# A recurrence and a gated MLP in one kernel: 16-bit ordering products and one lasting pair of accumulator banks

## The chip, the cores and the metric

The kernel runs on one core of a Trainium2 chip. The metric is the time of one execution on the device in microseconds (us), lower is better; where several were timed, the median is given. One further execution was recorded by the hardware profiler, and all rows below come from it. Its engines are called PE (matmul), PEld (the loading of weights into the PE array, which runs beside the matmuls), DVE (vector), ACT (scalar), POOL and SP (which issues the DMAs).

## What is computed

First a linear recurrence with a state of 48 x 48 for each of 4 sequences and 8 heads over 768 steps, then an MLP of 3072 rows, 384 to 2048 to 384, with a hard-swish gate:

```python
for t in range(S):
    kt, vt, rt, wt = (k[:, :, t], v[:, :, t], r[:, :, t], w[:, :, t])
    cur = np.einsum('bhd,bhe->bhde', u[None] * kt, vt)
    y[:, :, t] = np.einsum('bhd,bhde->bhe', rt, state + cur)
    state = wt[:, :, :, None] * state + np.einsum('bhd,bhe->bhde', kt, vt)
...
h = x @ w_in
relu6 = np.clip(h + 3.0, 0.0, 6.0)
g = h * relu6 / 6.0
return (g @ w_out).astype(np.float32)
```

All of it is in 32-bit floats.

## The kernel before

The recurrence is cut into 24 chunks of 128 steps (6 for each sequence, two sequences interleaved: chunks 0, 2, 4, ... 10 belong to one, 1, 3, ... 11 to the other, and 12 to 23 likewise). Each chunk consists of two halves of 64 steps (`a` = 0, 1). Eight heads are four pairs (`p`) of an even and an odd head (`g` = 0, 1). Features of even heads stand in partitions 0 to 47, those of odd heads in 64 to 111; partitions 48 to 63 are zero padding. So `PR` is 112, `GP` is 64, `D` is 48 and `HL` is 64.

For each chunk DVE makes decay products by scans (`back_scan`, `fore_scan`), PE multiplies keys by receptances (`score`, L500), DVE masks these into `A` (`above`), PE turns the keys (`turn_k`, L516) and ACT copies them out as `kn` (`turned_k`). PE then makes the **outer products** of keys and values that enter the state (`write`, L600). ACT copies them out as `kvs` (`written`, L611) and DVE adds them to the decayed state. The result of a chunk comes from **state products** (`read_state`, L578) and **value products** (`read_values`, L587), both added up in `y_ps`, from where ACT takes them as the MLP's input (`leave`, L685).

`y_ps` is a tile of two banks of the accumulator memory, one for each half `a`: columns 0 to 255 hold y of one chunk, columns 256 to 447 the outer products of the next. `new_y` allocates it anew for each read, in the same place, since the pool has one buffer of that name.

The MLP's matmuls for four chunks at a time (a block) fill the rest of PE's time: L718 and L737 for block 0, L833 (up) and L888 (down) for the five later ones, the latter with fewer products and more sums on DVE. The order of all steps is fixed by hand, in a long string (`ORDER`) that ranks them; each step issues its instructions in a fixed sequence on its engine. From chunk 4 on, one step (`read`) strings together, on PE: the 16 state products of chunk i, an **ordering product** (`mark`, L622), the 16 scores of chunk i + 1, a second ordering product, the 16 outer products of chunk i + 1 (8 if that chunk is one of the last two of its pair of sequences, 10, 11, 22 and 23), the 16 value products of chunk i, and the 4 transposes for chunk i + 2. Chunks 0 to 4 (`SOLO`) have their outer products in a step of their own (`write_alone`), and chunk 1 has these and y in other banks (`APART`, `KV_APART`).

An ordering product multiplies a 64 x 64 part of the identity by four of its columns, into a small tile `ps` that nobody reads. It makes PE's later products wait until the earlier ones are done, where both go to the same banks from different parts of the array. Each f32 matmul shows in the trace as two weight loads and two matmuls.

The outer product's weights are `kn[half, p, cols]`: 64 rows (steps of the half), and as columns the features, 0 to 63 for an even head (48 and the 16 of padding) and 64 to 111 for an odd one. The padding's columns write zeros to partitions 48 to 63 of `y_ps`, which ACT's copy of 112 partitions (L611) reads along.

Of the kernel before, what the change touches and what calls it, by code (L numbers as in the profile page):

```python
# [8 lines left out]
F32 = mybir.dt.float32  # L9
# [4 lines left out]
BF16 = mybir.dt.bfloat16  # L14
# [7 lines left out]
HL = L // 2  # L22
GP = 64
# [15 lines left out]
KV_APART = (1,)  # L39
# [205 lines left out]
def fast_path(tc, feat, tok, wflat, ub, ug, moe_w_in, moe_w_out, out, flag, n_chunks):  # L245
# [5 lines left out]
    nc = tc.nc  # L251
    NT, PR, nf = feat.shape[0], ug.shape[0], feat.shape[2]
    HD = tok.shape[3]
    D = PR - GP
    H = HD // D
    P = H // 2
# [11 lines left out]
    with ExitStack() as ctx:  # L268
# [3 lines left out]
        pp = ctx.enter_context(tc.tile_pool(name="pp", bufs=1, space=PSUM))  # L272
# [10 lines left out]
        def is_last(i):  # L283
            return i % NSEQ >= NSEQ - 2
# [6 lines left out]
        ident = const.tile([128, 128], F32, name="ident")  # L291
# [8 lines left out]
        u_bc = const.tile([128, HD], F32, name="u_bc")  # L300
        w_in = const.tile([128, NFC // 2, NCC, 2, 128], F32, name="w_in")
        w_out = const.tile([128, NFC, DM], F32, name="w_out")

        def constants():

            nc.vector.memset(back, 0.0)
            nc.vector.memset(back[:, :, HL:], 1.0)
            for b in starts:
                nc.vector.memset(b, 0.0)
            nc.vector.memset(three, 3.0)  # L310
            nc.vector.memset(ones, 1.0)
            make_identity(nc, ident)
            nc.gpsimd.tensor_add(eyes, ident[:, :HL], ident[:, HL:])

            mask_f = wk.tile([128, HL], F32, name="clip")
            nc.gpsimd.memset(mask_f, 1.0)
            for a in range(2):
                nc.gpsimd.affine_select(out=mask_f[a * HL:(a + 1) * HL], in_=mask_f[a * HL:(a + 1) * HL],
                                        compare_op=ALU.is_gt, fill=0.0, base=0, pattern=[[1, HL]], channel_multiplier=-1)
            nc.gpsimd.tensor_copy(out=mask, in_=mask_f)  # L320

            for _ in range(4):
                spin()

            new_x(0)
            x3_0 = blocks[0]["x3"]
            sel = blocks[0]["sel"] = wk.tile([PR, NCC, 128], F32, name="S_", bufs=1)
            nc.gpsimd.memset(x3_0, 0.0)
            nc.gpsimd.memset(sel, 0.0)
            for g in range(2):  # L330
                nc.gpsimd.tensor_copy(out=sel[:, :, g * GP + D:g * GP + D + X3],
                                      in_=ident[0:PR, g * GP:g * GP + D].rearrange("q (j r) -> q j r", j=NCC))

        def new_x(bk):

            x = wk.tile([128, NCC + 1, MB], F32, name="xT")
            blocks[bk].update(xT=x, x3=x[:PR, NCC])
# [213 lines left out]
        def new_y(i, alone=False):  # L551
            started = set()
            if i == APART and not alone:
                st[i].update(started=started, y_ps=[bank()[:, :P * HL].rearrange("q (p t) -> q p t", p=P) for _ in range(2)])
                return
            y_ps = pp.tile([128, 2, 512], F32, name="y_ps")
            if not alone:
                y_ = y_ps[:, :, :P * HL].rearrange("q a (p t) -> q a p t", p=P)
                st[i].update(started=started, y_ps=[y_[:, a] for a in range(2)], y_all=y_)
            j = i if alone else i + 1  # L560
            if j < NT and (alone or j not in SOLO):
                st[j]["kv_started"] = started
                st[j]["kv_ps"] = y_ps[:PR, :, P * HL:P * (HL + D)].rearrange("q a (p e) -> q a p e", p=P)
# [26 lines left out]
        def write(i):  # L590
            d = st[i]
            for p in range(P):
                for a in range(1 if is_last(i) else 2):
                    for g in range(2):

                        half = slice(a * HL, (a + 1) * HL)
                        cols = slice(g * GP, GP if g == 0 else PR)
                        fresh = (a, g * GP) not in d["kv_started"]
                        d["kv_started"].add((a, g * GP))
                        nc.tensor.matmul(d["kv_ps"][a][cols, p, :] if i in KV_APART else d["kv_ps"][cols, a, p, :], lhsT=d["kn"][half, p, cols],  # L600
                                         rhs=d["v"][half, 2 * p + g, :], start=fresh, stop=True, skip_group_check=True)
# [12 lines left out]
        def write_alone(i):  # L614
            if i in KV_APART:
                st[i].update(kv_started=set(), kv_ps=[bank()[:PR, :P * D].rearrange("q (p e) -> q p e", p=P) for _ in range(2)])
            else:
                new_y(i, True)
            write(i)

        def mark():
            nc.tensor.matmul(pp.tile([HL, 4], F32, name="ps"), lhsT=ident[HL:, HL:], rhs=ident[HL:, :4], start=True, stop=True)  # L622

        def read(i):

            new_y(i)
            read_state(i, range(P))
            if i + 1 < NT:
                mark()
                score(i + 1)  # L630
                mark()
                write(i + 1)
            else:
                nc.tensor.drain()
            read_values(i, range(P))
            if i + 2 < NT:
                turn_k(i + 2)
# [12 lines left out]
        def clear_y(i):  # L650
            new_y(i)
            for a in range(2):
                nc.tensor.matmul(st[i]["y_ps"][a], lhsT=ident[0:PR, :], rhs=blocks[0]["x3"][:, BY_SUM * L:BY_SUM * L + P * HL],
                                 start=True, stop=False, skip_group_check=True)
            st[i]["started"].update((a, g * GP) for a in range(2) for g in range(2))
# [54 lines left out]
        def bank(name="bank"):  # L710
            return pp.tile([128, 512], F32, name=name, bufs=4 if name == "bank" else 1)
# [451 lines left out]
        for bk in range(NB):  # L1163
# [7 lines left out]
            for d in range(2 * (bk > 0)):  # L1171
                at = K + U_ / 2 * d
                u, r = f"up{bk}.{d}.", f"read{bk}.{d}."
                name = lambda x: u + str(x) if isinstance(x, int) else r + x
# [41 lines left out]
            for p in range(2 * (bk > 0)):  # L1216
# [28 lines left out]
                for c, ((soon, s0), (late, l0)) in enumerate(((("c11", 0), ("c12", DM // 2)), (("c22", DM // 2), ("c21", 0)))):  # L1245
                    name = f"store{bk}.{2 * p + c}"
# [6 lines left out]
        for k, (which, j) in enumerate(vets):  # L1253
            i = 8 + k // 2
# [10 lines left out]
        def spin():  # L1265

            n_ = spins[0] = spins[0] + 1
            at = n_ % 4 * L
            nc.tensor.matmul(still[:, at:at + L], lhsT=ident, rhs=ident, start=n_ == 0, stop=True, skip_group_check=True)  # L1269
# [7 lines left out]
        plan.spin, plan.hint = spin, hint  # L1277
        plan.hint_at = f"down{NB - 1}.1.3.0"
        constants()
        plan.emit()  # L1280

# [237 lines left out]
def kernel(  # L1519
# [25 lines left out]
    flags = ctx.enter_context(tc.tile_pool(name="flags", bufs=1))  # L1545
    flag = flags.tile([1, 1], I32, name="flag")
    fast_path(tc, feat, tok, wflat, ub, ug, moe_w_in, moe_w_out, out, flag, n_chunks)
    bad = nc.values_load(flag[0:1, 0:1], min_val=0, max_val=128)
    with tc.If(bad > 0, preferred_fallthrough_block=True, label="general"):
# [68 lines left out]
```

## Time and profile before

| what | before |
|---|---|
| median of 3 timed runs | 536.13 us (535.11 to 536.87) |
| span of the profiled execution, first to last instruction | 533.3 us |
| granted PE clock | 1.000 |
| L622, ordering products: passes (loads), duration of one load | 76, 134 ns |
| L600, outer products into `y_ps`: passes | 672 |
| L578, state products into `y_ps`: passes | 688 |
| L587, value products into `y_ps`: passes | 736 |

The profiled execution is told by its span alone; the timed runs lie 2.8 us above it, for what happens ahead of the first instruction and behind the last. A load's duration is the time that one load spends under way; loads of the four quadrants of the array overlap, so that the distance between loads, not their duration, tells how fast they follow each other. In a timeline row stand the start, the length from the first start to the last end of the merged instructions, the engine, the line, the operation, the tiles, rows * columns of the weights, the shape, the count, and in brackets the idle time ahead with what ended it.

### The profile page before, as it was taken

The page shows a single profiled execution, that of the slowest core. Times are in us where ns is not written, and L with a number is a line of the kernel's source. Part 1 is how long each engine was busy: PE and PEld are TensorE (multiplying, and loading weights), DVE is VectorE, ACT ScalarE, POOL GpSimd, SP SyncE. Part 2 cuts the span into 40 slices and gives each one's busy share as a digit, 9 for nine tenths or more (in the row PEclk, how much of TensorE's full clock was granted, in tenths as well). Part 3 has the DMA queues.
Part 4 walks back from the last instruction along what each step waited for, and adds up shares of the span by engine and source line. Part 5 has one row for each costly group of instructions (what it writes and reads, how often), then busy time and mean ns, then how long its engine had stood idle before and what let it go on. Part 6 is the DMA issues. An engine that isn't in the chain of part 4 may idle for free.

```text
span 533.3 us, 13527 instructions
## 1 busy us (share of the span) xinstructions
PE 527.5 (99%) x5630; PEld 471.5 (88%) x5630; DVE 421.9 (79%) x741; ACT 263.8 (49%) x657; POOL 88.7 (17%) x79
## 2 busy tenths in 40 slices
PE   8999999999999999999999999999999999999997
PEld 8888877766888999988999988999988999988997
DVE  8989999877999977899677999886758855458740
ACT  4999886542356314474434466524245454253400
POOL 2000002450303033220432312114020000000000
PEclk9999999999999999999999999999999999999999
DMA  8958653343003535644324748122710000100001
GB/s 326 354 172 341 241 181 120 125 163 103 31 17 139 165 115 198 235 161 123 102 75 154 248 166 262 40 78 97 244 58 0 1 10 15 54 2 0 9 2 54
DMA packets 21458, 66.42 MB, mean 125 GB/s; under 512 B 3312, under 2 KB 11408, under 8 KB 21392
## 3 DMA queue, kind: packets, MB, share of 16 engines
q1 hardware_dynamic: 21264, 65.50, 35.8%
q8 instruction: 46, 0.75, 0.6%
q14 instruction: 20, 0.16, 0.1%
q10 hardware_dynamic: 128, 0.00, 0.0%
HBM read 59.69 MB, written 4.72 MB: 121 GB/s over the span
## 4 chain that ended last, share of the span: by engine, by line
PE 93%; DVE 4%; issue 1%; ACT 1%; DMA 1%; DVEq 0%; ACTq 0%
PE bank L888 29%; PE bank L833 25%; PE bank L737 8%; PE bank L718 7%; PE bankS L888 5%; PE bankS L833 4%; PE y_ps L578 3%; PE y_ps L587 2%; PE bank L500 2%; PE ps L516 2%; PE y_ps L600 2%; PE bankS L1269 1%; PE ps L475 1%; DVE g L858 1%; DVE g L850 1%
## 5 line engine op out<-in xcount | busy, mean ns | idle before, releaser
L854 ACT ACTIVATE clip<-g,three 128x512 f32<-128x512 f32 x80 | 56.5, 720 | 47.0 <-DVE g L850 29.9
L850 DVE TENSOR_TENSOR g<-bank,g 128x512 f32<-128x512 f32 x80 | 54.1, 685 | 22.3 <-PE bank L833 21.2
L858 DVE SCALAR_TENSOR_TENSOR g<-clip,g 128x512 f32<-128x512 f32 x80 | 57.3, 732 | 1.8 <-ACT clip L854 1.5
L888 PE MATMUL bank<-w_out,g 128*128 128x192 f32 x320 | 56.6, 326 | 0.0
L491 ACT ACTIVATE A<-eyes,dg 128x64 f32<-128x64 f32 x192 | 50.1, 339 | 9.2 <-PE y_ps L587 8.9
L450 POOL TENSOR_TENSOR K<-feat_in,E 112x512 f32<-112x512 f32 x17 | 24.9, 1466 | 175.0 <-PE ps L622 150.1
L888 PEld LDWEIGHTS bank<-w_out,g 128*128 128x128 f32 x320 | 52.9, 190 | 0.4
L718 PE MATMUL bank<-xT,w_in 128*128 128x256 f32 (+1 forms) x216 | 45.3, 361 | 0.2 <-DVE w_in L417 0.2
L454 POOL TENSOR_TENSOR W<-feat_in,W 112x512 f32<-112x512 f32 x17 | 22.8, 1341 | 125.7 <-DVE W L439 125.7
L737 PE MATMUL bank<-w_out,g 128*128 128x384 f32 x128 | 43.4, 488 | 0.0
L848 ACT COPY g<-bank 128x512 f32<-128x512 f32 x50 | 28.4, 584 | 30.3 <-PE bank L833 30.3
L718 PEld LDWEIGHTS bank<-xT,w_in 128*128 128x128 f32 x216 | 36.7, 190 | 5.4 <-PE bank L718 0.5
L833 PE MATMUL bank<-xT,w_in 128*128 128x256 f32 x160 | 40.5, 380 | 0.1
L685 ACT COPY xT<-y_ps 48x256 f32<-48x256 f32 x88 | 32.2, 366 | 13.9 <-PE y_ps L587 13.0
L906 ACT ACTIVATE o<-bank 128x192 f32<-128x192 f32 x30 | 9.5, 329 | 56.2 <-PE bank L888 56.1
L737 PEld LDWEIGHTS bank<-w_out,g 128*128 128x128 f32 x128 | 23.8, 190 | 14.3 <-DVE w_out L417 0.2
L439 DVE TENSOR_TENSOR_SCAN W<-feat_in,start 112x520 f32<-112x520 f32 x24 | 29.6, 1232 | 5.9 <-PE ps L622 5.8
L833 PEld LDWEIGHTS bank<-xT,w_in 128*128 128x128 f32 x160 | 30.2, 190 | 4.4 <-DVE g L850 0.5
L430 DVE TENSOR_TENSOR_SCAN E<-feat_in,back 112x520 f32<-112x520 f32 x24 | 30.2, 1258 | 1.2 <-DMA feat_in<-in_feat_dram 1.1
L833 PE MATMUL bank<-xT,bits 128*128 128x256 f32 x120 | 30.4, 380 | 0.0
L466 POOL TENSOR_TENSOR rk<-rk_in 128x384 f32<-128x384 f32 x15 | 21.0, 1402 | 46.4 <-DVE dg L483 29.2
L888 PE MATMUL bankS<-w_out,g 128*128 128x192 f32 x160 | 28.6, 327 | 0.0
(288 smaller groups left out, 1132.5 us busy)
## 6 DMA issues: line engine op xcount, KB each, us to landing
feat_in<-in_feat_dram SPq DMA_DIRECT2D x23, 772.5 KB, 4.7
bits<-in_moe_w_in_dram SPq DMA_DIRECT2D x8, 768.0 KB, 6.6
bits<-in_moe_w_out_dram SPq DMA_DIRECT2D x8, 768.0 KB, 6.0
feat_in<-in_moe_w_in_dram SPq DMA_DIRECT2D x8, 768.0 KB, 4.7
feat_in<-in_moe_w_out_dram SPq DMA_DIRECT2D x8, 768.0 KB, 4.9
rk_in<-in_tok_dram SPq DMA_DIRECT2D x15, 384.0 KB, 5.0
v_in<-in_tok_dram SPq DMA_DIRECT2D x24, 192.0 KB, 4.6
feat_in<-in_wflat_dram SPq DMA_DIRECT2D x6, 768.0 KB, 5.3
```

The lines of the kernel that those rows point to most:

```text
L430: nc.vector.tensor_tensor_scan(out=E_[:, ::-1], data0=d["w"][:, :0:-1], data1=back.rearrange("q p t -> q (p t)")[:, ::-1], initial=0.0, op ...
L439: nc.vector.tensor_tensor_scan(out=W_, data0=d["w"][:, :-1], data1=starts[i % 2].rearrange("q p t -> q (p t)"), initial=0.0, op0=ALU.mult, ...
L491: nc.scalar.activation(out=d["A"][:, h, :], in_=eyes, func=ACT.Copy, scale=d["dg"][:, h])
L685: nc.scalar.copy(out=blocks[bk]["xT"][g * GP:g * GP + D, :, at:at + HL], in_=st[i]["y_ps"][a][(g ^ a) * GP:(g ^ a) * GP + D, :, :])
L718: nc.tensor.matmul(h_ps[:, :(c1 - c0) * L], lhsT=w_in[:, f // 2, j, f % 2, :], rhs=b["xT"][:, j, c0 * L:c1 * L], start=(j == 0), stop=(j = ...
L737: nc.tensor.matmul(b["o", c][:, :DM], lhsT=g_of(0, f, c), rhs=w_out[:, f, :], start=(f == 0), stop=(f == NFC - 1))
L833: nc.tensor.matmul(b["p", d, c][:, z * HB:(z + 1) * HB], lhsT=weight(W_PLACE[r], d)[:, z, :], rhs=x_at(bk, X_PLACE[r]), start=fresh and z ...
L848: nc.scalar.copy(out=out_, in_=src)
L850: nc.vector.tensor_tensor(out=out_, in0=src, in1=out_of(bk, d, other), op=ALU.add if sign > 0 else ALU.subtract)
L854: nc.scalar.activation(out=c, in_=out_of(bk, d, u), func=ACT.Relu, bias=three, scale=twice)
L858: nc.vector.scalar_tensor_tensor(out=g, in0=blocks[bk]["r", d, u], scalar=6.0, in1=g, op0=ALU.min, op1=ALU.mult)
L888: nc.tensor.matmul(b["d", p, to][:, :h], lhsT=a, rhs=w(), start=(f == 0 and k in (1, 5)), stop=(f == HF - 1 and k in (2, 3, 4)), skip_grou ...
```

## The change

Three edits. The ordering product is made from the identity's bits read as 16-bit floats: 64 rows, 34 columns (34 rather than 64 output rows), in one pass. `y_ps` is allocated once, ahead of all work, and DVE clears partitions 0 to 111 of its columns from 256 on, in both banks, among the first memsets. And an even head's weights in the outer product are its 48 columns alone, except for chunk 1, whose other banks are not cleared.

```diff
+        y_ps = pp.tile([128, 2, 512], F32, name="y_ps")
...
+            nc.vector.memset(y_ps[:PR, :, P * HL:], 0.0)
...
-            y_ps = pp.tile([128, 2, 512], F32, name="y_ps")
             if not alone:
                 y_ = y_ps[:, :, :P * HL].rearrange("q a (p t) -> q a p t", p=P)
...
-                        cols = slice(g * GP, GP if g == 0 else PR)
+                        cols = slice(g * GP, GP if g == 0 and i in KV_APART else g * GP + D)
...
         def mark():
-            nc.tensor.matmul(pp.tile([HL, 4], F32, name="ps"), lhsT=ident[HL:, HL:], rhs=ident[HL:, :4], start=True, stop=True)
+            bits = ident.bitcast(BF16)[HL:]
+            nc.tensor.matmul(pp.tile([HL // 2 + 2, 4], F32, name="ps"), lhsT=bits[:, :HL // 2 + 2], rhs=bits[:, :4], start=True, stop=True)
```

On PE, read 11 (the block at 199.84 us of the trace) stands before as follows, from its state products to the first outer products (out<-in, output rows x columns, and in brackets the engines or DMA queues whose semaphores are waited for):

```order
L578 MATMUL y_ps<-W,S 48x64 [waits PE_49,Activation_49]
L578 MATMUL y_ps<-W,S 48x64
L578 MATMUL y_ps<-W,S 48x64 [waits DVE_49]
L578 MATMUL y_ps<-W,S 48x64 x13
L622 MATMUL ps<-ident 64x4 [waits PE_49]
L500 MATMUL bank<-W,K 64x64 [waits Pool_49]
L500 MATMUL bank<-W,K 64x64 [waits Activation_49]
L500 MATMUL bank<-W,K 64x64 x14
L622 MATMUL ps<-ident 64x4 [waits PE_49]
L600 MATMUL y_ps<-v_in,kn 64x48 [waits DMAHW3_49]
L600 MATMUL y_ps<-v_in,kn 48x48
```

and now, at the same place (the lines are one or two further down in the file):

```order
L579 MATMUL y_ps<-W,S 48x64 [waits Activation_49]
L579 MATMUL y_ps<-W,S 48x64
L579 MATMUL y_ps<-W,S 48x64 [waits DVE_49]
L579 MATMUL y_ps<-W,S 48x64 x13
L624 LDWEIGHTS ident
L624 MATMUL ps<-ident 34x4 [waits PE_49]
L502 MATMUL bank<-W,K 64x64 [waits Pool_49]
L502 MATMUL bank<-W,K 64x64 [waits Activation_49]
L502 MATMUL bank<-W,K 64x64 x14
L624 LDWEIGHTS ident
L624 MATMUL ps<-ident 34x4 [waits PE_49]
L601 MATMUL y_ps<-v_in,kn 48x48 [waits DMAHW3_49]
```

Nothing has moved. The first state product no longer waits for PE's own earlier work (13 of the reads lose that wait; read 10 had none), an ordering product is now a load and a matmul as two instructions, and all outer products have 48 rows. Behind the last read two up products (L833) of the last block gain a wait for PE.

On DVE, the start of the program before:

```order
L306 MEMSET back 112x520
L307 MEMSET back 112x8 [waits DVE_49]
L309 MEMSET start_79 112x520
L309 MEMSET start_80 112x520
L310 MEMSET three 128x1
L311 MEMSET ones 128x1
L430 SCALAR_TENSOR_TENSOR E<-feat_in,back 112x520 [waits DMAHW1_49,DVE_49]
```

and now:

```order
L307 MEMSET back 112x520
L308 MEMSET back 112x8 [waits DVE_49]
L310 MEMSET start_79 112x520
L310 MEMSET start_80 112x520
L311 MEMSET y_ps 112x2x256
L312 MEMSET three 128x1
L313 MEMSET ones 128x1
L432 SCALAR_TENSOR_TENSOR E<-feat_in,back 112x520 [waits DMAHW1_49,DVE_49]
```

One memset of 512 columns stands ahead of the first scan.

## Prediction

> **What bounds the kernel now.** I read the page first: busy shares, the slices with the granted clock, and the chain of waits.
>
> ```profile
> span 533.3 us, 13527 instructions
> PE 527.5 (99%) x5630; PEld 471.5 (88%) x5630; DVE 421.9 (79%) x741; ACT 263.8 (49%) x657; POOL 88.7 (17%) x79
> PEclk9999999999999999999999999999999999999999
> PE 93%; DVE 4%; issue 1%; ACT 1%; DMA 1%; DVEq 0%; ACTq 0%
> ```
>
> TensorE (PE) has the clock all along and is 93% of the chain that ended last, so a time taken out of its stream shortens the end, except ahead of a place where PE stood waiting. Of those the timeline of weight loads (PEld) has three after the start-up that matter, and the timeline of VectorE (DVE) one that belongs to them:
>
> ```profile
> 40.06 0.51 PEld L718 LDWEIGHTS bank<-xT,w_in 128*128 128x128 f32 x3 [0.54 <-PE bank L718]
> 171.94 0.19 PEld L833 LDWEIGHTS bank<-xT,w_in 128*128 128x128 f32 x1 [0.51 <-DVE g L850]
> 268.98 0.30 PEld L888 LDWEIGHTS bank<-w_out,S__2969 128*128 128x128 f32 x2 [0.62 <-DVE S__2969 L873]
> 123.97 1.24 DVE L439 TENSOR_TENSOR_SCAN W<-feat_in,start 112x520 f32<-112x520 f32 x1 [2.68 <-PE ps L622]
> ```
>
> What is gained before 40 us meets the first wait, and I count it as lost. At 171.94 and 268.98 PE waits for DVE, but DVE itself had waited for PE shortly before (2.68 us at 123.97), so both move forward together and little is lost.
>
> The change sits in the read blocks. The weight loads of read 11, a typical one (start, length, line, rows*columns of the weights, count):
>
> ```profile
> 199.84 0.52 PEld L578 LDWEIGHTS y_ps<-W,S 48*48 48x48 f32 x32 [0.23 <-issue]
> 200.29 0.13 PEld L622 LDWEIGHTS ps<-ident 64*64 64x64 f32 x1
> 200.35 0.13 PEld L622 LDWEIGHTS ps<-ident 64*64 64x64 f32 x1
> 200.35 0.60 PEld L500 LDWEIGHTS bank<-W,K 48*64 48x64 f32 x30
> 200.81 0.19 PEld L600 LDWEIGHTS y_ps<-v_in,kn 64*64 64x64 f32 x4
> 200.87 0.19 PEld L622 LDWEIGHTS ps<-ident 64*64 64x64 f32 x2
> 201.34 0.14 PEld L600 LDWEIGHTS y_ps<-v_in,kn 64*64 64x64 f32 x1
> 201.40 0.14 PEld L600 LDWEIGHTS y_ps<-v_in,kn 64*64 64x64 f32 x1
> 202.03 0.39 PEld L516 LDWEIGHTS ps<-ident,K 112*128 112x128 f32 x4
> 189.47 0.52 PEld L578 LDWEIGHTS y_ps<-W,S 48*48 48x48 f32 x32 [0.23 <-issue]
> 191.49 0.39 PEld L516 LDWEIGHTS ps<-ident,K 112*128 112x128 f32 x4
> 54.27 0.55 PEld L600 LDWEIGHTS y_ps<-v_in,kn 64*64 64x64 f32 x32 [0.33 <-issue]
> ```
>
> From L578 to L516 the block takes 202.03 − 199.84 = 2.19 us. The two rows at 189.47 and 191.49 are read 10, whose outer products are half as many (chunk 11 is the last of its sequence): 2.02 us. The row at 54.27 is the outer products of chunk 4, alone.
>
> Each f32 matmul shows as two passes (load and matmul), 32 loads for 16 matmuls. Weights of at most 64 rows and 64 columns sit in one of four quadrants of the array, called here by row half and column half: A (0,0), B (0,1), C (1,0), D (1,1). 32 loads in 0.5 us can only be four quadrants working side by side, 8 passes each. That gives **pass times**: with 64 weight columns (row at 54.27) (550 − 135) / 7 = 59 ns, as between the two L600 loads at 201.34 and 201.40; with 48 weight columns and 64 moving ones (L578, 0.52 us) (520 − 120) / 7 = 57 ns. So the longer of 64 loaded or 64 streamed columns sets a pass, and one of 48 and 48 should take about 48/64 of either, 44 ns.
>
> Per quadrant a full read block is: state products 8 × 57, scores 8 × 59, outer products 8 × 59 in A and C (even heads) but 8 × 44 in B and D, values 8 × 57; and C alone carries the two ordering products, 2 × 2 passes of 59. C: 16 × 57 + 20 × 59 = 2092 ns. A: 16 × 57 + 16 × 59 = 1856 ns. With 0.1 us until the array is empty for L516, C gives the 2.19 us of the trace: **C sets the block's length**.
>
> **The change part by part.**
>
> *Ordering products.* 19 reads (4 to 22) issue two each: 76 passes before (a pass per load row), 38 after. Before, a pair of passes cost C 2 × 59 = 118 ns. After, there is one pass of 34 columns; by columns 34/64 × 59 = 31 ns. No row of this kernel shows a 16-bit product, so I bound it: no cheaper than 0, no dearer than the 118 ns that it replaces if it merely keeps its place (a drain is a rival, below). I take 31, nearest to what load rows give per column. C loses 2 × 87 = 174 ns per block.
>
> *Even heads' outer products.* 8 passes go from 59 to 44 ns in A and in C: 120 ns each. Bounds: 0 if the pass is held by something other than its columns, 8 × 16 = 128 if the last column counts in full.
>
> *Together, a full block.* C goes to 16 × 57 + 8 × 59 + 2 × 31 + 8 × 44 = 1798 ns, A to 1736: C remains the longest, 0.29 us shorter. A little of it does not come through. Products are handed out in program order and a quadrant holds few in waiting: A's first outer product loads at 200.81, just before C's second ordering load at 200.87, although A had done its scores some 0.1 us earlier. With faster passes the quadrants meet at such places more often. I take 0.25 us, between 0.20 and 0.29, for 15 full blocks: 3.75 us.
>
> *Half blocks* (reads 9, 10, 21, 22). C has no outer products, A is longest: 1.86 + 0.1 = 1.96 of the 2.02 us, and the other 0.06 is A waiting behind C's ordering products. A loses 0.12, and of the 0.06 some 0.04: 0.16 us, four times, 0.64 us (bounds 0.12 and 0.18 each).
>
> *Outer products alone* (chunks 0, 2, 3, 4): 0.12 us each; three lie before the wait at 40.06 and count nothing, chunk 4 at 54.27 counts 0.11.
>
> *The stall at 171.94.* After 123.97 DVE works on almost without a break, so what PE gains in reads 8 and 9 it partly waits away: −0.1 (0 to −0.4).
>
> *The memset* is 512 columns on DVE:
>
> ```profile
> 1.67 1.04 DVE L309 MEMSET start<- 112x520 f32 x2
> 3.82 1.30 DVE L430 TENSOR_TENSOR_SCAN E<-feat_in,back 112x520 f32<-112x520 f32 x1 [1.09 <-DMA feat_in<-in_feat_dram]
> ```
>
> Two of 520 columns took 1.04 us, so it is 0.52 us, inside the 1.09 us in which DVE waits for the first load. Cost 0; were the cover gone, 0.52.
>
> *Waits.* One lasting tile frees the first state product of 13 reads from a wait of PE for itself. Read 11 had that wait and read 10 had not, and both start after 0.23 us of idle. Worth 0, at most 0.05 us each way; the same for the two up products (L833) behind the last read that gain one. The ordering load becomes an instruction of its own; behind it on PE stand the scores or outer products, and its wait is for what C had done long before: 0.
>
> Sum: 3.75 + 0.64 + 0.11 − 0.1 = **4.4 us**, so the span goes from 533.3 to 528.9. The median of the timed runs is 536.1, 2.8 above the span, which lies around it and stays: **531.7 us**.
>
> A rule to weigh here is whether quadrants run apart at all.
>
> ```profile
> 212.07 0.27 PE L500 MATMUL bank<-W,K 48*64 48x64 f32 x1
> 212.12 0.22 PE L578 MATMUL y_ps<-W,S 48*48 48x64 f32 x2
> ```
>
> A score (L500) starts ahead of two state products (L578) that stand before it in the program: a quadrant that is done goes on alone. The Trainium skill, "TensorE: Matmul & The Clock Gate", section "The mechanism", says that matmuls are "pc-monotone in start AND end — strict FIFO, no reordering". By this rule the trace disagrees in this place, and the result that it would give is the second rival.
>
> **The rivals.**
>
> 1. *The switch between 32 and 16 bit stops the array (slower).* Before each ordering product all four quadrants run empty. Entering and leaving a read block shows such a stop: 0.23 us of idle loads before L578. At that price an ordering product costs 0.23 in place of 0.118 us, and now in all quadrants: 38 × 0.11 = 4.3 us lost against 15 × 0.12 + 4 × 0.12 = 2.3 us from the columns: 536.1 + 2.0 = 538.1. It turns slower when the stop passes 0.118 + 2.3 / 38 = 0.18 us. Against it: rows and columns stay inside the same quadrant; for it: no row here has both types. Chance 0.09. The Trainium skill, "TensorEngine Tiling (Array Packing)", section "Key Properties", lets a change of tiling mode drain the engine, "not just tile"; the 0.23 us agrees, and it names no change of type.
>
> 2. *Quadrants in lockstep.* Then every step costs what its slowest quadrant costs, in half blocks too: 19 × 0.29 = 5.6 us, 530.5. The half block's 2.02 against 2.19 us speaks against it, since in lockstep both would last the same. Chance 0.04.
>
> 3. *The ordering product stays dear* (one pass of 90 ns or more): it does not do what it says. Then columns alone count, 2.3 us, to 533.8; with no gain of the columns but cheap products, 15 × 0.12 + 4 × 0.04 = 2.0, to 534.1. Chance 0.16.
>
> 4. *DVE takes over.* If it is the bound from 124 to 172 us and around 240 us, four reads' gain is waited away: 4.4 − 1.0, to 532.7. The windows for it: DVE is near full there, but it waits for PE in between. Chance 0.13.
>
> The forecast itself, 531.2 to 532.3: chance 0.58.
>
> **How the numbers follow.** Forecast, lockstep and DVE lie between 530.5 and 532.7 and hold 0.75; the dear product at 533.8 to 534.1 brings it to 0.91, less what other runs of a kernel spread. The bounds of the block, 0.20 and 0.29 us, are 15 × 0.05 and 15 × 0.04 us either way. I give 530.3 to 534.3. Faster by over 0.3% means under 534.5, about what a measurement of this kernel can tell from no change: 0.58 + 0.04 + 0.13 and most of rival 3, 0.84. Same 0.09 (the rest of rival 3, and a mild stop), slower 0.07.
>
> **What would show it.** In the profile after: a full block from state products to the transposes of 1.94 us, a half block of 1.86; L600's loads all 48 columns, 32 of them alone in 0.43 us; one ordering load per product, the next score in C some 31 ns behind it. If there is idle before each ordering product in all quadrants, rival 1 holds; if the wait at 171.94 grows by more than 0.4 us, rival 4. If blocks shrink as said and the end does not move by 4 us, the step from PE's stream to the end was wrong.

## The result, and the profile after

| | before | after |
|---|---|---|
| median of 6 timed runs each | 535.91 us (535.11 to 537.10) | 532.58 us (531.56 to 532.86) |
| ratio, 95% interval | | 0.9928 (0.9913 to 0.9943) |
| span of the profiled execution | 533.3 us | 531.0 us |

The forecast was 531.7 us in a range of 530.3 to 534.3, so the kernel became faster by 0.72% where 0.83% was forecast. Where a run lists both its time and its span, 1.8 to 2.1 us lie between them (532.86 and 531.0 us for the profiled one of the changed kernel), not the 2.8 us that the forecast reckoned with. So the profiled execution of the kernel before must have been one of its quickest, some 535.2 us, while 532.86 is the slowest of the six of the changed kernel: the spans fell by 2.3 us, the medians by 3.3. The page of the changed kernel, first its busy shares and the chain of waits:

```profile
span 531.0 us, 13439 instructions
PE 524.2 (99%) x5592; PEld 468.0 (88%) x5592; DVE 423.2 (80%) x742; ACT 263.7 (50%) x657; POOL 90.4 (17%) x79
PE 93%; DVE 4%; issue 1%; ACT 1%; POOL 0%; POOLq 0%; DVEq 0%; ACTq 0%
```

PE has the same shares in a shorter span: the bound is where it was. Then the weight loads of read 11, and behind them the first row and the last of read 10, the half block (lines are one or two further down now, so L579 is the state product, L624 the ordering product, L502 the score, L601 the outer product, L588 the value product, L518 the transpose):

```profile
198.96 0.52 PEld L579 LDWEIGHTS y_ps<-W,S 48*48 48x48 f32 x32 [0.23 <-issue]
199.42 0.09 PEld L624 LDWEIGHTS <-ident 64*34 64x34 bf16 x1
199.42 0.55 PEld L502 LDWEIGHTS bank<-W,K 48*64 48x64 f32 x30
199.94 0.10 PEld L624 LDWEIGHTS <-ident 64*34 64x34 bf16 x1
199.94 0.45 PEld L601 LDWEIGHTS y_ps<-v_in,kn 64*48 64x48 f32 x28
200.94 0.39 PEld L518 LDWEIGHTS ps<-ident,K 112*128 112x128 f32 x4
188.74 0.52 PEld L579 LDWEIGHTS y_ps<-W,S 48*48 48x48 f32 x32 [0.23 <-issue]
190.62 0.30 PEld L518 LDWEIGHTS ps<-ident,K 112*128 112x128 f32 x3
54.79 0.45 PEld L601 LDWEIGHTS y_ps<-v_in,kn 64*48 64x48 f32 x32 [0.33 <-issue]
```

By these rounded starts the full block lasts 200.94 − 198.96 = 1.98 us, 2.19 before; the half block 1.88, 2.02 before; the outer products of chunk 4, alone, 0.45 us, 0.55 before. One load stands in place of two for each ordering product, and these outer products' loads are all of 48 columns. The idle time ahead of the first state product is the same 0.23 us, with its wait gone. The two waits of PE for DVE that lie in the middle have not grown:

```profile
171.22 0.51 PEld L835 LDWEIGHTS bank<-xT,w_in 128*128 128x128 f32 x3 [0.51 <-DVE g L852]
267.51 0.46 PEld L890 LDWEIGHTS bank<-w_out,S__2955 128*128 128x128 f32 x3 [0.62 <-DVE S__2955 L875]
```

And the memset has its place inside DVE's wait for the first load of data; the first scan starts where it did (3.82 us before):

```profile
2.81 0.48 DVE L311 MEMSET y_ps<- 112x512 f32 x1
3.80 1.31 DVE L432 TENSOR_TENSOR_SCAN E<-feat_in,back 112x520 f32<-112x520 f32 x1 [0.44 <-DMA feat_in<-in_feat_dram]
```

The trace has starts to the nanosecond, and in these two runs block lengths (first load of the transposes minus first load of the state products) repeat within some 2 ns among like reads (reads 12 and 13, first chunks with half the state products, are some 14 ns shorter). So the experiments are read from the **median length of the 15 full blocks and of the half blocks** (three of the four: no transposes follow read 22), where the time of an execution spreads over 1 to 3 us. Before: 2199 and 2020 ns. Changed: 1974 and 1872 ns, so −225 and −148, and 15 × 0.225 + 4 × 0.148 + 0.10 (chunk 4) = 4.07 us if the fourth half block gained as much as the other three.

The two recorded spans differ by 2.3 us only. The rest lies at both ends. Ahead of the blocks the same 32 warm-up products took longer in this execution:

```profile
1.43 5.58 PE L1269 MATMUL bankS<-ident 128*128 128x128 f32 x32 [1.43 <-POOL ident masks.py:199]
...
1.43 6.58 PE L1271 MATMUL bankS<-ident 128*128 128x128 f32 x32 [1.43 <-POOL ident masks.py:199]
```

(first the kernel before, then the changed one). Their starts follow each other by 213 ns at first and by 111 ns later; before, that turned at 5.0 us, here at 7.1. That put the first read 0.56 us later. In e8 below, another execution of the changed kernel, they took 5.47 us. Another 1.1 us came behind PE's last product, where only an ACT copy and the last output DMAs are left: the last state products start 3.43 us earlier than before (443.89 against 447.32 us), and so do PE's last products (524.10 against 527.53), but the span ends only 2.3 us earlier.

### The profile page after: what moved, and what is told of

Its sections match the earlier page's. It is cut to its first block, busy times and chain, and to the rows that moved or that the text cites. A ratio compares the mean times of both kernels' runs of the same rounds, so it can differ in the third digit from the quotient of the medians.

```text
span 531.0 us, 13439 instructions
## 1 busy us (share of the span) xinstructions
PE 524.2 (99%) x5592; PEld 468.0 (88%) x5592; DVE 423.2 (80%) x742; ACT 263.7 (50%) x657; POOL 90.4 (17%) x79
## 4 chain that ended last, share of the span: by engine, by line
PE 93%; DVE 4%; issue 1%; ACT 1%; POOL 0%; POOLq 0%; DVEq 0%; ACTq 0%
PE bank L890 29%; PE bank L835 25%; PE bank L739 8%; PE bank L720 7%; PE bankS L890 5%; PE bankS L835 4%; PE y_ps L579 2%; PE bankS L1271 2%; PE y_ps L588 2%; PE ps L518 2%; PE bank L502 2%; PE y_ps L601 1%; DVE g L852 1%; DVE g L860 1%; PE ps L477 1%
## 5 line engine op out<-in xcount | busy, mean ns | idle before, releaser
L468 POOL TENSOR_TENSOR rk<-rk_in 128x384 f32<-128x384 f32 x15 | 22.2, 1479 | 44.5 <-DVE dg L485 28.4
```

## Experiments

The theory tested, formed after the result: a read block lasts as long as the longest of the four quadrants of the array (A to D), each of which works through its own passes. A pass right behind a product that streams 64 columns takes no less than that product's 57 ns, however short its own load is. The rivals: all quadrants go in lockstep; the number of columns alone sets an ordering product's time; the switch of types costs a stop; the waits that fell away are the gain. Each diff is against the changed kernel; the ratios are to the kernel before on the same chip, and "one run" means that there is a single execution, with no interval.

| run | full block, ns | half block, ns | ratio to before, 95% interval |
|---|---|---|---|
| before | 2199 | 2020 | 1 |
| changed | 1974 | 1872 | 0.9928 (0.9913 to 0.9943) |
| e1 products only | 2080 | 1944 | 0.9962 (0.9946 to 0.9978) |
| e2 columns only | 2092 | 1928 | 0.9955 (0.9939 to 0.9971) |
| e3 product of 64 columns | 1974 | 1872 | one run |
| e4 products twice | 2025 | 1928 | one run |
| e5 lasting tile only | 2198 | 2019 | 1.0004 (0.9993 to 1.0015) |
| e6 second product in D | 1966 | 1872 | 0.9918 (0.9902 to 0.9934) |
| e7 f32, 34 columns | 2041 | 1927 | one run |
| e8 changed again | 1974 | 1873 | 0.9920 (0.9904 to 0.9936) |
| e9 products in A | 1962 | 1953 | one run |

**e1, the ordering products alone** (the lasting tile stays):

```diff
-                        cols = slice(g * GP, GP if g == 0 and i in KV_APART else g * GP + D)
+                        cols = slice(g * GP, GP if g == 0 else PR)
```

> The 16-bit ordering products and the lasting tile stay, even heads' outer products load 64 columns again. Before, a full read block (first state product to the transposes) lasts 2.20 us and a half one 2.02; with the change 1.974 and 1.872. Quadrant theory (a block lasts as long as its longest quadrant; a pass right behind a product that streams 64 columns takes no less than 57 ns, however short its own load, so an ordering product saves one pass of two, not 87 ns of 118): 2.08 and 1.96, so about 15 x 0.12 + 4 x 0.06 = 2.0 us off the time. Rival, the prediction's own term (31 ns for the product): 2.03 in a full block. Rival, the gain is all in the columns: 2.20 and 2.02, no time off.

Full blocks lost 119 ns, half ones 76. In full blocks that is about 60 ns a product, not 87, and the quadrant theory's number; half ones lost 16 ns more than it said.

**e2, the columns alone:**

```diff
-            bits = ident.bitcast(BF16)[HL:]
-            nc.tensor.matmul(pp.tile([HL // 2 + 2, 4], F32, name="ps"), lhsT=bits[:, :HL // 2 + 2], rhs=bits[:, :4], start=True, stop=True)
+            nc.tensor.matmul(pp.tile([HL, 4], F32, name="ps"), lhsT=ident[HL:, HL:], rhs=ident[HL:, :4], start=True, stop=True)
```

> The ordering products are two f32 passes of 64 columns again; the 48 columns and the lasting tile stay. Quadrant theory: 2.08 to 2.09 in a full block, 1.92 to 1.93 in a half one, about 15 x 0.11 + 4 x 0.10 = 2.0 us off the time. Rival, the gain is all in the products: 2.20 and 2.02. If the two edits hide each other, this and the products alone add up to more or less than 0.225 us.

−107 and −92 ns, as expected. With e1 that makes −226 and −168, against −225 and −148 of both: in full blocks the edits add up, in half blocks they share 20 ns.

**e3, a 16-bit product of 64 columns:**

```diff
-            nc.tensor.matmul(pp.tile([HL // 2 + 2, 4], F32, name="ps"), lhsT=bits[:, :HL // 2 + 2], rhs=bits[:, :4], start=True, stop=True)
+            nc.tensor.matmul(pp.tile([HL, 4], F32, name="ps"), lhsT=bits[:, :HL], rhs=bits[:, :4], start=True, stop=True)
```

> As the changed kernel, but the 16-bit ordering product loads 64 columns, not 34. Quadrant theory: the pass is held at 57 ns by the 64 columns streamed ahead of it, so the block stays at 1.974 to 1.98 us. Rival, the product's columns set its time: 2 x 27 ns more, 2.03 us.

```profile
199.21 0.52 PEld L579 LDWEIGHTS y_ps<-W,S 48*48 48x48 f32 x32 [0.23 <-issue]
199.66 0.10 PEld L624 LDWEIGHTS <-ident 64*64 64x64 bf16 x1
200.19 0.11 PEld L624 LDWEIGHTS <-ident 64*64 64x64 bf16 x1
201.18 0.40 PEld L518 LDWEIGHTS ps<-ident,K 112*128 112x128 f32 x4
```

The loads are 64 columns wide, and the block is 1974 ns as with 34. The product's width costs nothing here; going from two passes to one is the whole gain. That fits the theory, by which the product ahead is still streaming while this one loads.

**e4, each product twice:**

```diff
+            m = pp.tile([HL // 2 + 2, 4], F32, name="ps")
+            for _ in range(2):
+                nc.tensor.matmul(m, lhsT=bits[:, :HL // 2 + 2], rhs=bits[:, :4], start=True, stop=True)
```

> As the changed kernel, but each 16-bit ordering product is issued twice in a row. Quadrant theory: the second one stands behind a product of 4 columns, so it takes its load's 31 ns: 2.036 us in a full block, 1.93 in a half one. Rival, any such pass takes 57 ns: 2.09. Rival, going between 32 and 16 bits stops the array: the second brings no further switch and costs next to nothing, 1.98, while the first already holds the stop.

Both loads of the first pair in read 11:

```profile
199.18 0.09 PEld L626 LDWEIGHTS <-ident 64*34 64x34 bf16 x1
199.24 0.10 PEld L626 LDWEIGHTS <-ident 64*34 64x34 bf16 x1
```

+51 ns in a full block, so 25.5 ns for a second product behind a first of 4 columns (31 expected, 57 for the rival). The second load starts 0.06 us behind the first, as with 64 columns before (200.29 and 200.35): it is the step behind the second load that is short. Half blocks: +56, as expected (1.93 us). Yet by the passes alone C has time to spare there; so a product in C is not free in a half block. A's outer products stand behind it in program order, and the forecast had them wait for it.

**e7, one f32 product of 34 columns**, two passes:

```diff
-            bits = ident.bitcast(BF16)[HL:]
-            nc.tensor.matmul(pp.tile([HL // 2 + 2, 4], F32, name="ps"), lhsT=bits[:, :HL // 2 + 2], rhs=bits[:, :4], start=True, stop=True)
+            nc.tensor.matmul(pp.tile([HL // 2 + 2, 4], F32, name="ps"), lhsT=ident[HL:, :HL // 2 + 2], rhs=ident[HL:, :4], start=True, stop=True)
```

> As the changed kernel, but the ordering product is f32 with 34 columns, two passes. Quadrant theory: as the 16-bit product issued twice, 2.036 us in a full block and 1.93 in a half one, since passes and columns count and the type does not. Rival, the type counts (a 16-bit pass is cheaper than an f32 one of as many columns, or its switch costs): other than the doubled product by more than 0.02 us.

2041 ns: the second f32 pass costs (2041 − 1974) / 2 = 33.5 ns, 8 more than the second 16-bit one in e4. The difference of the blocks, 16 ns, is below the 20 that were set as the mark. So the type is worth little beside the number of passes. And e7 takes no switch of types at all where e4 takes four per read, yet its blocks are no shorter: no stop at a switch shows.

**e5, the lasting tile and its memset alone** (the diffs of e1 and e2 together).

> The lasting tile and its memset alone: f32 ordering products of 64 columns, even heads load 64 columns. Both theories of the quadrants: blocks of 2.20 and 2.02 us, no time off (within 0.3%). Rival, the waits of PE for itself that fall away are worth something: up to 13 x 0.05 = 0.65 us off, seen as less idle ahead of the first state product (0.23 us before).

2198 and 2019 ns, ratio 1.0004: the 13 waits and the memset are worth nothing that can be seen.

**e6, the second product in quadrant D:**

```diff
-        def mark():
+        def mark(odd=False):
...
+            out_ = pp.tile([HL + n, 4], F32, name="ps")[HL:] if odd else pp.tile([n, 4], F32, name="ps")
...
                 score(i + 1)
-                mark()
+                mark(odd=True)
```

> As the changed kernel, but the second ordering product of each read writes partitions 64 to 97, so it runs in quadrant D (second row half, second column half), not in C as the first does. Quadrant theory: C is the longest by 0.044 us after the change, so a full block goes from 1.974 to 1.93 us, a half one stays at 1.87; 15 x 0.044 = 0.66 us off the changed kernel's time. Rival, lockstep (every step costs its slowest quadrant, wherever the product runs): blocks as in the changed kernel, no time off.

Full blocks of 1966 ns, only 8 less, where 44 were expected and 0 from lockstep: most lie nearer to the rival. But they are of two kinds; here are reads 11 and 15, two full blocks of this run:

```profile
199.03 0.52 PEld L579 LDWEIGHTS y_ps<-W,S 48*48 48x48 f32 x32 [0.23 <-issue]
200.97 0.39 PEld L518 LDWEIGHTS ps<-ident,K 112*128 112x128 f32 x4
...
280.62 0.52 PEld L579 LDWEIGHTS y_ps<-W,S 48*48 48x48 f32 x32 [0.23 <-issue]
282.59 0.40 PEld L518 LDWEIGHTS ps<-ident,K 112*128 112x128 f32 x4
```

Reads 11, 13, 14 and 19 are some 32 ns shorter than in the changed kernel (1.94 us; read 13, a first chunk, 1.93) and the other eleven only some 8 ns (1.97 us; read 12, a first chunk, 1.95), from the same sequence of instructions. Something beside the longest quadrant holds the block then, probably the order in which the products are handed out; that is argued, not shown. In time the run cannot be told from the changed kernel (0.9918 and 0.9920 on the same chip).

**e8** is the changed kernel once more, for that comparison.

> The changed kernel once more, on the chip of these runs: blocks of 1.974 and 1.872 us, 3.3 us off the time of before.

Its median was 531.39 us against 535.69 of before on that chip, −4.3 us (0.80%): 1 us more than expected, from the same blocks (1974 and 1873 ns).

**e9, both products in quadrant A:**

```diff
-            bits = ident.bitcast(BF16)[HL:]
+            bits = ident.bitcast(BF16)[:HL]
```

> As the changed kernel, but both ordering products take rows 0 to 63 of the identity, so they run in quadrant A (first row half, first column half) and not in C. Quadrant theory: in a full block A and C carry the same passes, so A is now the longest and the block stays within 0.02 us of 1.974; in a half block, where C has no outer products and the ordering products cost nothing there, A has both: 1.872 + 0.10 = 1.97 us. Rival, lockstep (a step costs its slowest quadrant, wherever the product runs): both blocks as in the changed kernel, 1.974 and 1.872.

Read 10, a half block, of this run:

```profile
188.08 0.52 PEld L579 LDWEIGHTS y_ps<-W,S 48*48 48x48 f32 x32 [0.23 <-issue]
188.52 0.09 PEld L624 LDWEIGHTS <-ident 64*34 64x34 bf16 x1
189.04 0.10 PEld L624 LDWEIGHTS <-ident 64*34 64x34 bf16 x1
190.04 0.39 PEld L518 LDWEIGHTS ps<-ident,K 112*128 112x128 f32 x4
```

1.96 us against 1.88 with the products in C: +81 ns (98 expected), while full blocks went to 1962, −12 (some to 1952, as in e6 of more than one kind). Lockstep would have left both alone. Where a product runs decides what it costs: in a half block it is 81 ns dearer in A than in C.

Reads 12 and 13 are the clearest case, and the expectation did not name them. As first chunks they leave out the state products of quadrants A and D (`read_state`), so that here A has time to spare for the ordering products. Read 13 of this run:

```profile
247.93 0.39 PEld L579 LDWEIGHTS y_ps<-W,S 48*48 48x48 f32 x12 [0.33 <-issue]
249.80 0.39 PEld L518 LDWEIGHTS ps<-ident,K 112*128 112x128 f32 x4
```

1870 ns, and 1895 in read 12, against some 1960 for both in the changed kernel: with C relieved and A not longer, the block is 91 and 65 ns shorter, where lockstep says 0. Why the two reads differ is not known.

## Why the prediction was right, step by step

- **C sets the block's length, and quadrants run apart.** Shown: e9 lengthens half blocks, leaves most full ones nearly alone and shortens reads 12 and 13, by a change of quadrant alone. Before, these two reads gave A eight passes fewer and were only some 14 ns shorter (2185 against 2199), so A was not the bound. As a bound the longest quadrant is not complete: in e6, with C relieved, blocks fell by some 8 or 32 ns and not by 44.
- **The ordering product at 31 ns.** This is the term that was mis-sized. In a full block it takes 118 − 60 = 58 ns: e1 gains 60 ns a product instead of 87, and e3's 64 columns take as long as 34. The reading that fits both, and the 0.06 us between the two loads of e4, is argued from them: a load runs beside the product ahead of it, and the load behind it finds no room before that product has streamed its 64 columns. Only a second short product in a row costs about what the columns say (25.5 ns in e4, 33.5 in e7).
- **Even heads' products, 120 ns in C.** e2 gave 107 in a full block and 92 in a half one; alone, chunk 4's took 0.10 us less, 0.11 forecast. The 44 ns for a pass of 48 columns were a little low: by that row it is (450 − 120) / 7 = 47 ns.
- **A loss of 0.04 us per block where quadrants meet.** Not there as such: the forecast took 0.25 of 0.29, and 0.225 is what the two measured terms add up to (119 + 107 = 226). The cut was made for the wrong reason, and by luck it covered most of the error in the two terms above (294 forecast for both).
- **Half blocks 0.16 us.** Measured 0.148, but not by the parts given: A's columns alone gave 92 ns and not 120 (e2), the products alone 76 where 60 was to be the most (e1). The total was right in part by luck.
- **The stall at 171.94, −0.1.** The wait stayed at 0.51 us: DVE came earlier by as much as PE. Nothing was lost.
- **Memset, waits, the load as an instruction of its own: 0.** e5 bears out the memset and the waits. The load as its own instruction has no run of its own; the 119 ns of e1, one whole pass for each product, leave nothing over for it in full blocks.
- **The sum.** 4.4 forecast; 15 × 0.225 + 4 × 0.148 + 0.10 = 4.07 by the blocks; 3.3 and 4.3 us in the two sets of timed runs. The end moved by less than 4 us in the first set, but PE's last products did come 3.43 us earlier though the first read came 0.56 us later: together 3.99 of the 4.07 us. So the step from PE's stream to the end held, and what differed lay ahead of the blocks and behind them.
- **The median as the span and 2.8 us.** The gap of one execution is some 1.9 us. The forecast span, 528.9, was 2.1 us below the recorded 531.0, the forecast median only 0.9 us below the measured one. The other 1.2 us is luck again: the recorded span lay 2.8 us below the median before, and 1.6 us below it after.
- **The rivals.** A stop at each switch: excluded by e1, where the 16-bit products make each full block 119 ns shorter and not longer, and by e7, which has no switch and is not shorter than e4 (e4 alone does not decide it, since doubling a product adds no switch). Lockstep: excluded by e9. A product that stays dear: half true, some 58 ns, between the 31 of the forecast and the 90 of the rival. DVE taking over: the two waits are as they were.

## What to carry to other kernels

Where products use a quarter of the array each, add up the passes of every quadrant and shorten the longest; a product that only has to be there costs less in a quadrant with time to spare (81 ns less in a half block of e9), though not nothing (e4 added 56 ns to half blocks). A rule that fits these runs: a pass costs the longest of its own load, its own streaming and the streaming of the product ahead of it, so counting columns alone overstates what a narrower load saves. Small gains show in the length of a repeated block to the nanosecond where the time of an execution spreads over one to three microseconds.

## What the runs showed of the hardware that was not expected

- A load of 34 columns behind a product that streams 64 is no cheaper than one of 64 (e3: 1974 ns both ways). By the full blocks, a 16-bit pass behind a product of 4 columns took 25.5 ns and an f32 pass of the same width 33.5. The Trainium skill, "TensorE: Matmul & The Clock Gate", section "Wait — 56ns, not 53.3ns?", gives about 25 ns as the least distance between starts, however few the columns. The 25.5 ns of e4 agree with it.
- 16-bit and 32-bit products stood beside and behind each other in one quadrant, and no stop shows for it: full blocks with four switches last 2025 ns (e4), with no switch and as many passes 2041 (e7).
- The same instructions can give two block lengths in one execution, 1.94 and 1.97 us (e6); why is open.
- The change of the warm-up products' pace from 213 to 111 ns came between 4.2 and 7.4 us in the recorded executions (e7 and e3), and with it the 32 products took between 5.2 and 6.7 us; in the changed kernel's record the first read came 0.56 us later than before.
